# Two steps for the largest absolute K, six unread products, and the last segment turned by TensorE, under a new stored order

## The chip, the cores and the metric

The kernel runs on one core of one Trainium2 chip. Its engines work side by side, each through its own queue in order: TensorE (PE; its weight loads are listed as PEld), VectorE (DVE), ScalarE (ACT), GpSimd (POOL) and SyncE (SP, which here only issues DMAs). The metric is the device time of one execution in microseconds.

## The reference

Two independent layers on 2048 tokens of width 640; their outputs stand side by side. Layer A is a gated long convolution, layer B attention over four segments of 512 tokens with a memory carried between segments. Cut to what matters:

```python
# A: short filter on k (4 taps), times v, a causal convolution of length 2048 per channel, times q
k_shift = sum(k_pad[:, t:t + S] * shift_k[:, ks - 1 - t] for t in range(ks))
kv = k_shift * v
y = irfft(rfft(kv, 2 * S) * rfft(ssm_k, 2 * S))[:S] + kv * ssm_D
a = q * y
# B: 32 heads of 20, segments s = 0..3 of 512 tokens
q, k, v = x @ wq, x @ wk, x @ wv
p = softmax(qs @ ks.T * scale + causal_mask)
a_dot = p @ vs
a_mem = (phi(qs) @ M) / (phi(qs) @ z + 1e-6)      # phi(t) = t + 1 if t > 0 else exp(t)
o = g * a_mem + (1 - g) * a_dot                   # g = sigmoid(beta) per head
M, z = M + phi(ks).T @ vs, z + phi(ks).sum()
b = o @ wo
```

## The kernel before, in words

Layer A runs over five blocks of 128 channels (`conv`, `dp` 0 to 4). Each block loads and turns its filter, applies the short filter as seven shifted products with diagonal matrices (`ks`), multiplies by v (`vt`), transforms data and filter by products with cosine tables (`spectrum`: eight groups of four products into PSUM, each evicted by ACT to `F`, then sums and differences on DVE), multiplies the spectra on DVE (`product`: many `tensor_tensor` of 1024 to 4096 elements per partition), transforms back (`inverse`: eight products per piece, then a DVE product with q, then two stores from POOL's queue). The per-channel weight `ssm_D` enters as one extra product in the filter's first spectrum piece (line 459), with `Drow`, a tile that is zero but for the weights in its first row, and a tile of ones.

Layer B runs over eight units: segment `u // 2`, half of the heads `u % 2`. `project` computes K, Q and V for four groups of 128 tokens (five accumulating products of 320 columns each), evicts them by ACT, turns K and Q together by a DMA transpose on SP into `KQT` (a head takes 32 rows, 20 of them used), and forms phi of both. For the softmax no maximum over the scores is taken. Instead each query gets an upper bound: the largest absolute K of every channel (`kam`, line 608), spread into a small matrix `A`, times the absolute turned Q (`qabs`); four small products give the bound, ACT evicts it to `bT`, and four small DMAs on SP write it into spare rows of the turned Q, so that the score products subtract it.

`attend` computes the scores in three kinds of blocks: A and J below the diagonal, D on it (with the mask added by further products). Four score tiles run side by side in the array, since a head has only 32 rows. ACT takes the exponential of 1024 columns at a time into one of seven `ET` buffers (160 times in all); then value products of 21 columns sum the result in PSUM, DVE divides (`rr`, `o2`) and writes `o_s`. `project_out` turns `o_s`, multiplies by `wo` and stores. For segments 0 to 2 the turn is a DMA transpose. For segment 3 the five blocks of 128 columns are treated in three parts (`PARTS`): the first three blocks by one DMA transpose for each group of 128 tokens, the fourth ("mid") and fifth ("last") by PE products with the identity matrix and an eviction that alternates between ACT and DVE. The first part needs the heads of the last unit's first group, the last part needs the very last heads.

The order of the work is not the order of the program. A recorder lists every operation (1501 of them, line 147) and every PSUM group, and `issue` (line 244) emits them in a stored order, a permutation packed into a text (`ORDER`, line 775); a second text (`BASE`, line 797) gives each PSUM group its bank out of eight. The planner that found the order is not part of the kernel; its costs are in `price` (line 190) and have no effect on the stored order. All instructions carry the line number 253 in the profile, for they are issued there; the tiles' names tell them apart. Each engine takes its operations strictly in the stored order, and an operation whose inputs or bank are not ready holds up everything behind it on its engine.

Of the kernel before, what the change touches and what calls it, by code (L numbers as in the profile page):

```python
# [104 lines left out]
class Recorder:  # L105
# [84 lines left out]
    def price(self, op, method, out, ins, dur):  # L190
# [8 lines left out]
        elif method in ("dma_start", "dma_start_transpose"):  # L199
# [3 lines left out]
            if method == "dma_start_transpose":  # L203
                packets, per = size / 256, 23.5
                op.dur = 5.1 * size / 1024
# [56 lines left out]
class Layer:  # L262
    def __init__(self, ctx, tc, A_q, A_k, A_v, A_shift_k, A_ssm_k, A_ssm_D, B_x, B_wq, B_wk, B_wv, B_wo, B_beta, out):
# [52 lines left out]
        nc.gpsimd.dma_start(out=self.Drow[0:1, :], in_=self.ssm_D[None, :])  # L316
# [61 lines left out]
    def conv(self, dp):  # L378
# [56 lines left out]
        def spectrum(kind, src):  # L435
            F = self.ring("F", [128, 4, 2, 512], n=FBUF)
            summed = kind == "X" and dp in PEX
            for c in range(4):
# [4 lines left out]
                for i in range(2):  # L443
                    if i % FW == 0:
                        g = self.group(FW, "F")
                    with rec.one():
                        for j in range(2):
# [3 lines left out]
                            for h in range(2):  # L451
# [6 lines left out]
                                if last and h == 0:  # L458
                                    nc.tensor.matmul(o[:, 0:128], lhsT=self.ones[:], rhs=self.Drow[:, dsl], start=False, stop=False, grp=g, skip_group_check=True)
# [84 lines left out]


# [23 lines left out]
    def project(self, u):  # L569
# [5 lines left out]
        for t in range(4):  # L575
# [17 lines left out]
            for i, n in ((0, 4), (1, 2)):  # L593
# [135 lines left out]
    def project_out(self, s):  # L729
# [4 lines left out]
        for p in parts:  # L734
            for t in range(0, 4, n):
                rec.key = ("oT", s, t) + (() if p.stop == 5 else ("first",) if not p.start else ("mid",))
                o = self.o_s[s][:].rearrange("p t h d -> p t (h d)")
                if p.start:
# [4 lines left out]
                    self.evict((t + (p.stop == 5)) % 2, oT[:, t, p], g.ap[:, 0, 0:128 * (p.stop - p.start)].rearrange("p (c q) -> p c q", q=128), g)  # L743
# [29 lines left out]
SK_ACT, X_ACT, W_SP = (), False, ()  # L773
KQW, FW, WW = 1, 1, 1
ORDER = r"""
c-jrrgLW7S5Cy>9yLan0we8flZKt+v+qP{dwQbwBZR@>nm~$qrq!5vG5?#_uJc%qRC6#25jFMUcC9_PI88TBKCNU8~;z~pb5S6b&2``x>jpUL@5?>NX42dbRB(@}!#FA7JNiwM<NhG<XMHO+0h1`-&
(jkjfm8=p?vP%LaL=MR*$&mtCkQLeRT`Ef=e3QgThB%TEv5^XCP)G_(5h*GKq@a|N(vnB=N(m_`#iY38ll)Rf%1U}<KxU*yAmShilA^Z6M;$3AHKmqRlOU-saS;z0kqI@Vu{4o}(pnlxC@C)$rGnI#
Hqu<`$~<W)4Wy~mlk8|Ap(Tv8k^&fjoM<LJkpsEV3%PL<c~B5-rJW2!d+8vZWE_U0qm0K0OhZ0&k<OAAQ6#F2L{}+<Q5cJ<7=*#-jXvlm6EF-DF&(2Z2K_Mwvt_R2M_H6dIdqr8=pnN(1HEJjW@0G5
qc7^A9~!`I5<=Nz{6G;D!v}oC94U%V_>2e^(duKCL^m_qLM%d0`H3I$3;z(#!dnzuEK6ke|Af7zugt*$%*8@kB&ARqWw2D1$$VKL^AT3mqFNsrD#N6oR6s>6MkTD2Xf_Y9^%BEY$p%?28)b!Tl7?uE
{!$zz@l!U-02wHQqy}oD7HXpoN+71Kl}4zHDu`uOQ4LKHgu1AXb+Sd8Vz@Lzh^&zjvRZ<rIliDR+MzvKpcVe2CB9*Z43@3Z0Y@dQZIkWN5u>CvcF0aSD7z%G?Unr!PTF9kbjBe$ES<1Vy5P8U#cnwu  # L780
-OwF><d+<gV{%eX$ZzR^J#t#A>sOqTB{(Bz<(x#a0Q-$UI4>9El7zM}wg&6a(pp(3>uj+tuB}BE>uPbVkzJI=*3Oz+Z|h@&t%3ElB$m`#STAd618lrZka!l~5?gyqXvwUDtwu*1XrpC}jFSX5S*Az`
f^iUsa9OU%dL**3vH?`rNixWW*kNphsOkz#lT}!Wzw%Fp8nm`9#WI-I)8sbHuF7&um20vCJFyG9F;Vs)j7HF~8c}b^b-5`~HJXOfy$G$hB%I!s=o(&QXk?9~QM8T*XkFch$8rFhuo+vh72EJcj$l6;
>QOY(V>pGTdKzc39p`WyZLPmGvpaGgXK(@CteM`Ei?}O~<RtpqLpgyAmeG3HWn95kTtj#3XRR%hwXy4HVwZ3O59GeY)LUq32{o3cwRD!=5^Hizp^3D<p0NhnSd-{&G|`vxN?yxOeIs!+jV9ID8du|K
GQESlNMR{$q&<~q@?2g>DtnA4c!)=MinN+iQ)y}q)O0%BnrnK^Y+3Cd?&AUC>j=wY88oB*vrL*<v+5`tZDVb`J+&<Q%!FfXoTauj)=~qlmA26D_QN`AC;e*QEHrCsHp^}~ET`qQT-ILmS$^xFd-RRH
wU3tDYG^Ipss*f|6|th0#|qg;`6OTDt-O<BmQ4#=cKsl2wVig>E}B4#TMjK@IrTN(;In+P+?q@CXjko~`Lv|9);9XtUfFB=W4raQm9=tK-ty}+yq6bviMM!%=Xh+Ttc;bmC-w>xtb$dxDpu91S&&sU
r}3RtvYJNLvf5V1s#{&FVfE~#g<^fnt6@0NK3G^zvI6?s!n2@8WCRw{!usCYuq~h43!7roY^qgZRerI#Hs6|Zo+-g*Y{&L&&K8_ywYW>?*iWm?aGY*+INN60UM-^g^p{0qHO{cbw!|h|ab0T5te6(n
07heEF1HmHg>@OkMqFSG`5q;-q%N}38kGyJjF#2zy53gVY74dy+hCh)jjgouT29y6M%!$MwTJf99d<;kXeq6#TdbG%)}6M?`sh{*((Sg*_Ui%d#%g*{cUw(1<{{l@`|W@ow7z=CqI0P3wLNy!y6~8_
W&<|iaa(7H?Su`}&K#^m^rQ{cL3+ea*+?CwUD=(dtrO2$3=Y>G9HFCijP}>DI!*`ZHjT&ljLDX4#ql~pdvT&xXAMr$$vQ>ru|E5-1NSolPwR2*&Fy+ZPwFYn&NEs;r|D6xs8e;i&d?k@t2x<EXX-4S
t#fsb9@F!7!Om+(UeL>WMX%X)J7?$gqFu7fcE#rDRl8w*8JqnWhjDp>H`$Z@dDCuLWxdAh9KetK#DpBgL`=;4+@TNnlmod`Z`&QaYxnHFC1Fxl(qz1-cNvTKcuAk|8B;MelQShB*h70{?-|H6Ov`jk
!4F)fulSmInUDFIff<>J3p6vcFg@pMR=(g%F4D!iL>KCJUe#+_fCX8I*Y$?p(!wmtBFx1+ys7uKxaVeBmScH7)(R}f;(VyzSb`P#KufX|pXeif%o6^NPxY?e(`<aMFSIo8=rb+prTn$N(L#QQh5ajQ  # L790
`E%Cx;Vi>S9Kj#_$&sw$w^-F*>MQ-lKfKM~9Lw<>$K|?0SLsR}%)cDPe>AWBf5k)iR!4I=#o_PtgO1@^U8mDHoijL-Ls{N8=xv?F6<o<-Ea$WNUO(!3oxn+4t)CgJA^J%x_(Xo;WKLlNujEr%**EGY
{j5v4S-0q1F6BJV=K?O|GS1;5e$lV`P1oou26HtFctH<g4PV2xe8aa~$Fg42H*ym<a|^d}F}HC8ziVh;&oExyf9MYG<SrKTu)dpn7|tX3cJAd*-N$-f+RJ!-Kfv%F*$=XzH}YTVAfk9wZ|X%nq6c^#
uj`S#sMAAvV}Hm;tmZ-Pp2U-S6F<VE{H+x|nn(8-9@AraGmq`byt%jX*51-nd7!8ExE{~r`yWl<Ej*zo_mm#T6Zv0F>?e7O$9aP3J%wlT%$~)wdN$AQIXr`B^faE<5AiU&`acz<^PHZ`b9)}o>-jvt
clS2l&5zL#3ZVhC^>#keNBL;K%qzS|#c5t*d+*@k5FQcG(K~r(@8UhYr$<CoL_>7MKyUBkeZ8Oe_W?f8m-`qGgO%RP2l-$h;zNCy5BC*5!pHhJAMa;4!6*7zUgad8?B}@5&oeBhcqB~q=|00}`YfOA
0hr@+eV$+T>psor`vPC+i+r)K@m0Rg*ZUG*>#O~gAN9z%;lUo_SNyau^@D!MkNFng>YIGCpYtd<?-#huxBCX)=!gBdpYS7o#xM9uzv;L9s_*cNzSH;kHNWj={gUtXeZI?g`+h&*{{i6J>gE
"""
BASE = r"""
c-l=<0TRO?2#W~v{~r%R?7UtrB7_jE0XXn_vsQ;8%HCM?M0v7&S^L>p#c!S+o}I@7Ms@D4r;$)Gp@^V8p00sf7crc9MwDS=s?|&yHF(x6yH0Ws?gry9BUw2WW3-N#Z}ONm#jmTSSOx2Vh{m<m06m~(
{C1_W?mAZ2UWyK343ANEGxHE<D{eFMb~-f{tzc%VtLc16<0QLaU(VhjT`#N4_s}-^OkSs+CdDt}7GH?d?e22EI=Ha#b?)MLgp``gDCyrMl70Vqy7JGXtAChBvq)*Uc(TMa^qrdpX*;h!{hN?o7&GHw
tt3i{H;DLh`eWHMAOBQvRU9pyx<da-NK4n9_J@fH9gpYQn>RIeLzCE{=>tDfMh1%  # L800
# [8 lines left out]
def kernel(  # L809
# [63 lines left out]
```

## Time and profile before

| | |
|---|---|
| median of three runs | 290.04 us (289.86 to 291.36) |
| profiled execution | 290.99 us, its span 289.2 us |
| granted TensorE clock, mean | 0.987 |
| PE busy | 258.5 us, 4226 products |
| DVE busy | 262.0 us, 398 instructions |
| ACT busy | 254.0 us, 391 instructions |
| POOL busy | 42.5 us, 71 instructions |
| ACT's exponentials | 160, 155.9 us |
| DVE's reductions of the turned K | 8, 18.2 us |

Busy time is the time in which an engine has at least one instruction under way. Successive instructions of an engine can overlap a little, so the distance between two starts is often shorter than the first one's duration. A value in brackets at the end of a line of the timeline is the idle time before the instruction, with what ended it.

### The profile page before, as it was taken

To read this page: it belongs to the slowest core of one execution; us is meant where nothing else is said; L and a number is where in the kernel's file an instruction comes from. 1 tells how busy PE (TensorE), PEld (TensorE's weight loads), DVE (VectorE), ACT (ScalarE), POOL (GpSimd) and SP (SyncE) were. 2 spreads that over 40 slices of the span, in tenths; PEclk is the share of its full clock that TensorE was granted. 3 is DMA by queue.
4 is the path that set the end of the run, shared out by engine and by line. 5 is a ranking of instruction groups with operands and counts; after the bars stand their busy time and mean duration, and the time that the engine had idled before them with its cause. 6 is when DMAs were issued, how large, how long until landed. Compare 5 with 4: busy or idle time off the path is not lost. (4 is left out here: it accounts for less than half of the span.)

```text
span 289.2 us, 9883 instructions
## 1 busy us (share of the span) xinstructions
PE 258.5 (89%) x4226; PEld 195.3 (68%) x4226; DVE 262.0 (91%) x398; ACT 254.0 (88%) x391; POOL 42.5 (15%) x71
## 2 busy tenths in 40 slices
PE   0999998789989899999989999998799977888895
PEld 0788756668667678777656888656586755656673
DVE  0569999999999999999999999999999999989554
ACT  1694899899998978999999999999979999989972
POOL 8300000001005000403100310022001220001620
PEclk9999999999999989999999999999799999999999
DMA  6999889899943779916696149952492029921252
GB/s 190 383 243 178 217 160 174 207 215 164 223 118 85 165 99 204 205 61 120 166 167 144 43 59 174 191 133 71 88 156 57 24 55 141 207 26 48 58 123 91
DMA packets 113500, 40.71 MB, mean 141 GB/s; under 512 B 105696, under 2 KB 111376, under 8 KB 113328
## 3 DMA queue, kind: packets, MB, share of 16 engines
q1 hardware_dynamic: 108624, 34.07, 61.8%
q0 software_dynamic: 2064, 4.76, 5.5%
q10 hardware_dynamic: 2768, 1.24, 1.8%
q8 instruction: 33, 0.54, 0.8%
q14 instruction: 11, 0.09, 0.1%
HBM read 14.11 MB, written 5.24 MB: 67 GB/s over the span
## 5 line engine op out<-in xcount | busy, mean ns | idle before, releaser
L253 ACT ACTIVATE ET<-ps 128x1024 bf16<-128x1024 f32 x160 | 155.9, 1064 | 6.7 <-PE ps L253 6.4
L253 PEld LDWEIGHTS <-xT 128*128 128x128 bf16 x640 | 60.5, 99 | 32.2 <-issue 10.8
L253 PE MATMUL ps<-wqkv,xT 128*128 128x320 bf16 x480 | 75.5, 303 | 3.6 <-ACT ET L253 1.9
L253 ACT CAST F<-ps 128x512 bf16<-128x512 f32 x80 | 43.0, 614 | 4.2 <-DVE F L253 1.6
L253 POOL DMA_DIRECT2D out_dram<-outa x32 | 22.2, 815 | 165.1 <-DVE outa L253 141.1
L253 PEld LDWEIGHTS <-ET 128*128 128x128 bf16 x1296 | 40.3, 97 | 4.1 <-issue 2.2
L253 PE MATMUL ps<-Va,ET 128*128 128x21 bf16 x1280 | 41.2, 172 | 0.1
L253 PE MATMUL ps<-KQT 32*128 32x128 bf16 (+2 forms) x896 | 34.5, 242 | 2.0 <-ACT ET L253 1.0
L253 PEld LDWEIGHTS <-Wf 128*128 128x128 bf16 x320 | 29.9, 98 | 6.5 <-issue 2.4
L253 ACT CAST KQ<-ps 128x320 bf16<-128x320 f32 x64 | 27.5, 454 | 3.7 <-PE ps L253 3.1
L253 PE MATMUL ps<-wo,xT 128*128 128x320 bf16 x160 | 25.2, 299 | 1.1 <-ACT ET L253 0.6
L253 PEld LDWEIGHTS <-KQT 32*128 32x128 bf16 x896 | 16.5, 94 | 12.0 <-issue 10.8
L253 PE MATMUL ps<-skd,kr 128*128 128x128 bf16 (+3 forms) x140 | 20.9, 301 | 1.1 <-ACT ET L253 1.0
L253 PE MATMUL ps<-Y,Wi 128*128 128x256 bf16 x160 | 20.3, 273 | 1.7 <-ACT ET L253 1.0
L253 PE MATMUL ps<-vt,Wf 128*128 128x256 bf16 x160 | 20.1, 272 | 1.8 <-DVE vt L253 1.4
L253 PE MATMUL ps<-kT,Wf 128*128 128x256 bf16 x160 | 21.2, 276 | 0.0
L253 PEld LDWEIGHTS <-kr 128*128 128x128 bf16 x140 | 17.3, 146 | 5.5 <-issue 2.7
L253 DVE TENSOR_TENSOR o<-ps,rr 128x640 bf16<-128x640 f32 x24 | 19.7, 823 | 0.7
L253 PE MATMUL ps<-mright,mleft 32*128 32x128 bf16 x512 | 14.4, 219 | 6.5 <-ACT ET L253 3.4
L253 PE MATMUL ps<-Mbd,PqT 128*128 128x84 bf16 x96 | 18.2, 202 | 1.9 <-ACT ET L253 0.9
L253 DVE TENSOR_TENSOR Y<-Y,pq 128x2048 bf16<-128x2048 bf16 (+1 forms) x20 | 18.6, 949 | 0.1
L253 DVE TENSOR_TENSOR pq<-Xh,Kh 128x2048 bf16<-128x2048 bf16 x15 | 18.3, 1223 | 0.4
(77 smaller groups left out, 356.4 us busy)
## 6 DMA issues: line engine op xcount, KB each, us to landing
vt<-in_A_v_dram SPq DMA_DIRECT2D x10, 256.0 KB
pq<-in_A_q_dram SPq DMA_DIRECT2D x10, 256.0 KB
out_dram<-outa POOLq DMA_DIRECT2D x32, 64.0 KB, 2.5
out_dram<-outb POOLq DMA_DIRECT2D x12, 160.0 KB, 3.1
ET<-in_A_ssm_k_dram SPq DMA_DIRECT2D x3, 512.0 KB
Wf<-c_wf SPq DMA_DIRECT2D x2, 512.0 KB
Wi<-c_wi SPq DMA_DIRECT2D x1, 1024.0 KB
kT<-in_A_ssm_k_dram SPq DMA_DIRECT2D x2, 512.0 KB
```

The lines of the kernel that those rows point to most:

```text
L253: f(*[fix(a) for a in args], **{k: fix(v) for k, v in kw.items()})
```

## The change

- The largest absolute K is no longer reduced from the turned K. DVE takes the absolute value of the unturned K (a bit mask over 4 x 320 elements per partition), the maximum of token groups 0, 1 with 2, 3, and the maximum of the two that remain, written with zeroed pads into a new tile `kmax`. Four PE products with the identity turn it into a PSUM bank, and the reduction runs over that bank, 128 elements for each of four head groups. `qabs` and the rest stay.
- In segment 3 the first three blocks, too, are turned by PE (three products for each of four groups of 128 tokens) and evicted by DVE. Four DMA transposes leave SP's queue.
- Six products of the identity with 512 columns of `wo` write a PSUM bank that nobody reads (`keep_busy`).
- `Drow` becomes 128 by 128 with the weights of the five blocks in its rows 0 to 4; the product that adds them takes as its stationary operand one column of the identity repeated 128 times, and the tile of ones goes.
- The planner's cost of a DMA transpose gets a floor. This line acts on the planner alone.
- Both stored texts are new, for 1543 operations and 488 PSUM groups (470 before).

Unpacked and laid beside the old one, the new order has these marks. On PE, unit 2's turn of `kmax` stands among the second block's filter spectrum, unit 4's and 5's shortly after score and value products, unit 6's after a J block, unit 7's among V projections. Four of the unread products (2, 0, 3, 5) stand among the third block's data spectrum and unit 1's last score blocks, ahead of the fourth block's short filter; two (1, 4) stand between unit 5's last value products. At the start two more Q projections stand ahead of the first filter spectrum, the three new DVE steps of unit 0 ahead of its sums, one small `Mbd` product behind them. At the end one output projection of segment 2 moves from before the last inverse piece to between the last two groups of value products, and all eight three-product pieces of segment 3's projection come after the last value products, where before two of them came ahead. On SP, ACT, DVE and PE many neighbouring operations have changed places besides. The core of the diff:

```diff
-        self.Drow = c.tile([128, D], bf16, name="Drow")
-        self.ones = c.tile([128, 128], bf16, name="ones")
+        self.Drow = c.tile([128, 128], bf16, name="Drow")
+        self.kmax = c.tile([128, 16, 32], bf16, name="kmax")
...
-        nc.gpsimd.memset(self.ones[:], 1.0)
+        nc.gpsimd.memset(self.kmax[:, :, DH:32], 0.0)
...
-                                    nc.tensor.matmul(o[:, 0:128], lhsT=self.ones[:], rhs=self.Drow[:, dsl], ...)
+                                    nc.tensor.matmul(o[:, 0:128], lhsT=self.ident[:, dp:dp + 1].to_broadcast([128, 128]), rhs=self.Drow[:], ...)
...
+    def keep_busy(self):
+        for n in range(KEEP):
+            self.rec.key = ("keep", n)
+            g = self.group(1, "keep")
+            self.nc.tensor.matmul(g.ap[:, 0, :], lhsT=self.ident[:], rhs=self.wo[:, n % 5, 0:512], start=True, stop=True, grp=g)
...
+        rec.key = ("kmax", u)
+        ka = self.ring("qabs", [128, 4, L])[:].rearrange("p g q -> p (g q)")[:, 0:1280].rearrange("p (t h d) -> p t h d", t=4, h=16)
+        V.tensor_scalar(out=ka.bitcast(i16), in0=KQ[:, :, 0, :, 0:DH].bitcast(i16), scalar1=0x7fff, scalar2=None, op0=ALU.bitwise_and)
+        V.tensor_tensor(out=ka[:, 0:2], in0=ka[:, 0:2], in1=ka[:, 2:4], op=ALU.max)
+        V.tensor_tensor(out=self.kmax[:, :, 0:DH], in0=ka[:, 0], in1=ka[:, 1], op=ALU.max)
+        g = self.group(1, "kmax")
+        with rec.one():
+            for k in range(4):
+                nc.tensor.matmul(g.ap[:, 0, 128 * k:128 * k + 128], lhsT=self.kmax[:, 4 * k:4 * k + 4, :], rhs=self.ident[:], start=True, stop=True, grp=g)
         rec.key = ("bound", u)
         kam = self.ring("kam", [128, 4], f32, n=2)
-        V.tensor_reduce(out=kam[:], in_=KQT[:, 0], axis=AX.X, op=ALU.max, apply_absolute_value=True)
+        V.tensor_reduce(out=kam[:], in_=g.ap[:, 0, :].rearrange("p (k t) -> p k t", k=4), axis=AX.X, op=ALU.max, grp=g)
...
-                if p.start:
+                if len(parts) > 1:
                     g = self.group(1, "oT")
...
-                    self.evict((t + (p.stop == 5)) % 2, oT[:, t, p], ...)
-                elif len(parts) > 1:
-                    nc.sync.dma_start_transpose(out=oT[:, t, p], in_=o[:, t, 128 * p.start:128 * p.stop])
+                    self.evict(not p.start or (t + (p.stop == 5)) % 2, oT[:, t, p], ...)
...
+KEEP = 6
...
+    K.keep_busy()
```

More of the change, by code (lines that the diff above doesn't have):

```diff
@@ L204, in price @@
                 packets, per = size / 256, 23.5
-                op.dur = 5.1 * size / 1024
+                op.dur = max(1260, 5.1 * size / 1024)
                 op.lat = 1250.0 + (800.0 if dram else 0.0)
@@ L458, in spectrum @@
                                 if last and h == 0:
-                                    nc.tensor.matmul(o[:, 0:128], lhsT=self.ones[:], rhs=self.Drow[:, dsl], start=False, stop=False, grp=g, skip_group_check=True)
+                                    nc.tensor.matmul(o[:, 0:128], lhsT=self.ident[:, dp:dp + 1].to_broadcast([128, 128]), rhs=self.Drow[:], start=False, stop=False, grp=g, skip_group_check=True)
                     if i % FW == FW - 1:
@@ L742, in project_out @@
                             nc.tensor.matmul(g.ap[:, 0, 128 * (cc - p.start):128 * (cc - p.start) + 128], lhsT=o[:, t, 128 * cc:128 * cc + 128], rhs=self.ident[:], start=True, stop=True, grp=g)
-                    self.evict((t + (p.stop == 5)) % 2, oT[:, t, p], g.ap[:, 0, 0:128 * (p.stop - p.start)].rearrange("p (c q) -> p c q", q=128), g)
-                elif len(parts) > 1:
-                    nc.sync.dma_start_transpose(out=oT[:, t, p], in_=o[:, t, 128 * p.start:128 * p.stop])
+                    self.evict(not p.start or (t + (p.stop == 5)) % 2, oT[:, t, p], g.ap[:, 0, 0:128 * (p.stop - p.start)].rearrange("p (c q) -> p c q", q=128), g)
                 else:
@@ L779 @@
[L779 to L786, printed above, removed]
@@ new lines @@
+FD<BLwX^)zZZccC%Q&5_Go-v$)N<NWdPpysqZKp~BeReEkOdl!;rT;<YA7kD#Z^g`P$3wCQ5cnB*iaj5ST5I?Y@~B_p03b1oG<gWw+xnr8j^Emfh^K_vREr=Ul}5cWr-}5D!NF1%2KVYO*9l^v9>PL
+CE8!=XkA?@vDs8Zv!2%1xNM*$wV5uHeiDxZBmoCWe3sJ9Qd-x_dRZqcWtCLbYPwOXYYp8Z8>E9a*G<w<TWU=WmRdScT4+M9mNha|mdgqmCL^Sk4wp9CNfWWNcG0eSP`1i8X{~MbpSIK1jKPT9A=_oA
+?2<ovQVvUd?WWzehX&YFS88baBfI60{MFO4UyevGJs^8zuN;@e?5#=IhCw_k`(%}#krQ%Cj!9DfmS1vK&PiYP<9Ug|XpGJal8kNHjz;H2xg=Y3n|5MncHvg-%E27Mo}4I?Bso*C7gI77({Q71)=iq0
+qnM7p*@x*lnj>YDjFz!7PR7e+NzI`g#xd;A2{M3FWU`FoSSpC|oWSk6Lk)kW8pg;@J*kciJgtISn8;K5PbLvKpa*rGuGf$_q=z*WLSutoktnE(Ft{oKFc1kLa73dbGFIy~IjWNx0c&-Q-jJ|}i0cv_
@@ new lines @@
+wGo7yvP%&NhdS7;d-Rx|(7n1(Z^>iXuNFA2XEYFKfG2WW8se;8(sO!6uj)0ut~d0up4VVr(2LrGBY8)<aX4@4UAd)Aa9eXRH}A<Ey{q?h1e+oc@5>|U$nLza4<rEwauD0|fj-hZ?7)W-4bc%3^-v$#
+84r!n7(0=JIhhFYkq}Sir96{Y@<v|E3wbVykpxNcSTiycU+OE3f!K(JWO%KaIfYaCM&D{&q`-7O)8t5r=Q@pPkQS*>1F4Y?)$v51YI<bE49;X;=3`B4MMw)}bD5vB`G<cwi(mOdzfp~r0hzD|aS&u#
+n3Vy`#<$W8&Cvo8EQCe3ck)5rO92*SAr@v!bU<cwL=l=5XHk~m9F}A$mSbstlwvHyPm%>$kqz0A6FHCz6<Cp<<%^VOWmaN13va(zh1K|*Uo{WD>1S4Db=Kr({i0v^PHXUkzSocXN!y?;LR&3{wc4!9
+di=?<%#Fwfo5%WWz=n)!olq1-P=`&}h)vmy&DnyD*^*H#nzf?ae0D}&gs~WwAFa?D`4H1$TVcepg80rKjBD*s2wkuXyRm@n(G`ohgo_!=2HGHtXpyV{dRap2ZS8F}*YF?3npp>1%jVYK+FCmsU@fer
@@ L800 @@
-tt3i{H;DLh`eWHMAOBQvRU9pyx<da-NK4n9_J@fH9gpYQn>RIeLzCE{=>tDfMh1%
+c-l=<2@-@b42n7b|Kp87>rO{ob3te{b1O4Evn%Y`mHXZM<-1<Xti@o-eFr?Vr^4>A7d(lKT1)K;<vn-?JCOppwf;eD;AHZrJcdfXXI36miM5Av5<58)lQ^-fVRi7H%drtvh<K6ST$iWORl@(GJMv9W
+B4gl5Y4+yPe~=1YCO8f}tjrp&crr^x`o(h9K5Pd3OsAGcjqVC;AK;{vH`G4}CX5fAsD^lxnxmem46**XQG-AoyEPiUwAh*^hBr@dh+!$N#lgiPZnu6_2(fEab@gJpztL@<`#Sn_mN>}=#l-vIQiX(K
+k7g^NZGqi@F_j%D%~?DAOsu|&DK+{kU0|0|f;y)DlT)W}*7@o`1vs^Rl{wQo@;`Ty6L-(Qt~L2TW;X`U
 """
```

29 lines of the change are left out of this document (14 added, 15 removed).

## The prediction

> **What bounds the kernel now.** I read the busy times first, then the kernel in stretches, then the chain of waits, then single engines in order of time. The profiled execution took 290.99 us, its span is 289.2 us; the median of three runs is 290.04 us, 0.95 us less. All terms below are made against the profiled execution and the sum is then lowered by 0.95 us.
>
> The table by stretches has, after the length, the busy us of PE, weight loads, VectorE (DVE), ScalarE (ACT) and POOL, each with its number of instructions, then the granted clock.
>
> ```profile
> PE 258.5 (89%) x4226; PEld 195.3 (68%) x4226; DVE 262.0 (91%) x398; ACT 254.0 (88%) x391; POOL 42.5 (15%) x71
> ...
> 21.20:115.80 94.60, 88.46 (x1253) 67.69 (x1251) 93.47 (x135) 82.00 (x131) 5.59 (x8) 0.98 0.85 170
> 115.80:206.20 90.40, 84.92 (x1399) 62.78 (x1397) 89.56 (x129) 87.10 (x140) 15.49 (x24) 1.00 0.68 127
> 206.20:217.00 10.80, 10.80 (x179) 8.51 (x179) 10.66 (x19) 8.90 (x16) 0.00 (x0) 0.84 0.85 124
> 217.00:243.00 26.00, 22.29 (x488) 16.95 (x490) 25.36 (x40) 26.00 (x36) 5.52 (x8) 1.00 0.37 63
> 243.00:258.60 15.60, 13.12 (x303) 9.47 (x306) 14.55 (x23) 14.25 (x17) 0.00 (x0) 1.00 0.84 132
> 258.60:277.60 19.00, 16.62 (x373) 12.16 (x366) 14.30 (x26) 18.86 (x22) 5.83 (x9) 1.00 0.24 63
> 277.60:289.20 11.60, 8.40 (x136) 6.61 (x135) 5.70 (x15) 4.43 (x10) 1.95 (x3) 0.96 0.32 95
> ```
>
> The page's 91, 89 and 88 per cent look like three equal engines; the stretches do not. From 21.2 to 206.2 us DVE idles 1.13 + 0.84 us out of 185, so it sets the pace there. ACT idles 12.6 us before 115.8, but only 3.3 + 1.9 + 0 + 1.35 = 6.55 us from there to 258.6, and 0.14 us in the 19 us after. The end hangs on PE, as the chain of waits shows (start, length, what):
>
> ```profile
> 206.20 10.80 PE ps L253 x178
> ...
> 275.61 1.98 ACT ET L253 x2
> 277.59 0.04 issue
> 277.63 8.42 PE ps L253 x136
> 286.05 0.02 issue
> 286.07 0.43 ACT kT L253
> ```
>
> So: DVE until about 206, one PE piece, ACT's exponentials from 243 to 277.6, then 8.42 us of gapless PE. Work saved on DVE counts fully early, and later only as far as ACT can follow; work added in the last 8.42 us of PE counts in full.
>
> **The largest absolute K (eight times).** One reduction over 2048 turned elements of K goes. In its place come an absolute value of 1280 elements, a maximum of 640, a maximum of 320, four PE turns of 128 columns, and a reduction of 512 elements out of PSUM. Groups of DVE by shape (count, busy us, mean ns):
>
> ```profile
> L253 DVE TENSOR_REDUCE kam<-KQT 128x4 f32<-128x2048 bf16 x8 | 18.2, 2279 | 0.0
> L253 DVE TENSOR_SCALAR qabs<-KQ 128x1280 bf16<-128x1280 bf16 x6 | 2.8, 470 | 0.2
> L253 DVE TENSOR_TENSOR PP<-PP,qabs 128x640 bf16<-128x640 bf16 x12 | 5.8, 480 | 0.0
> L253 DVE TENSOR_TENSOR o_s<-o 128x320 bf16<-128x320 bf16 x24 | 7.1, 296 | 0.2
> L253 DVE TENSOR_TENSOR vt<-ps,vt 128x512 bf16<-128x512 f32 x20 | 13.1, 681 | 0.1
> ```
>
> The first three new steps have rows of their own size and pattern (the 1280-element row reads this same KQ layout). No reduction reads PSUM in this trace. Its lower end is a quarter of 2279, 570 ns; its upper end the same length read from PSUM beside a second operand, 681 ns; I take 0.68, the row nearest in source and length. What counts is the distance between starts:
>
> ```profile
> 29.12 2.28 DVE L253 TENSOR_REDUCE kam<-KQT 128x4 f32<-128x2048 bf16 x1
> 31.32 0.68 DVE L253 TENSOR_SCALAR qabs<-KQT 128x2048 int16<-128x2048 int16 x1
> ...
> 92.77 0.48 DVE L253 TENSOR_TENSOR PP<-PP,qabs 128x640 bf16<-128x640 bf16 x1
> 93.17 0.68 DVE L253 TENSOR_TENSOR vt<-ps,vt 128x512 bf16<-128x512 f32 x1
> 93.77 0.68 DVE L253 TENSOR_TENSOR skd<-ident,skc 128x512 bf16<-128x512 bf16 x1
> ```
>
> Each starts 0.08 us before the record in front ends (29.12 + 2.28 against 31.32; 92.77 + 0.48 against 93.17). So the old reduction occupies 2.20 us and the new four (0.47 + 0.48 + 0.30 + 0.68) - 4 x 0.08 = 1.61 us: 0.59 us saved per unit. A rule speaks against four for one: the Trainium skill, "VectorE: DVE Perf Modes", section "The DRAIN you can't avoid", says that the next op waits until the pipe is empty, and to keep the count of ops low (it adds that an op which is not held may start earlier). With whole records, 1.93 against 2.28, the six units would give 2.10 us and not 3.54, and the forecast, the other terms kept, would be 288.8 us; the starts above speak for the overlap.
>
> By the unpacked order, units 1 to 6 take this in the stretch that DVE bounds or shares: 6 x 0.59 = 3.54 us. Unit 0's first three steps now stand ahead of the first spectrum's sums, where DVE waits 1.73 us, and cost nothing (1.01 us); there the gain is 2.20 - 0.60 = 1.60 us. Were that wait gone, they would cost 1.01 us. Unit 7's lies after 243, under ACT: nothing. Together 5.14 us.
>
> **The start.** PE and ACT now take two more Q projections ahead of the first spectrum, and one small Mbd product falls behind it.
>
> ```profile
> 14.90 0.27 DVE L253 TENSOR_TENSOR Mbd<-ginv,epsrow 128x16 bf16<-128x16 f32 x1
> ...
> 21.19 1.23 DVE L253 TENSOR_TENSOR Kh<-F 128x2048 bf16<-128x2048 bf16 x1 [1.73 <-ACT F L253]
> ...
> 16.50 0.73 ACT L253 CAST KQ<-ps 128x320 bf16<-128x320 f32 x2
> 17.14 4.01 ACT L253 CAST F<-ps 128x512 bf16<-128x512 f32 x8
> ```
>
> Two evictions take ACT from 16.50 to 17.14, 0.64 us, in front of eight spectrum evictions that pace themselves; the product is 0.27 - 0.08 = 0.19 us. Cost: 0.83 us. On the load queue of SP one filter is swapped for another ahead of the tables: same bytes, zero. POOL's zeroing is reordered with one tile narrower and one new: zero, POOL being idle 85 per cent; if late, KQ's first transposes wait for it.
>
> **The rest of the new order.** Elsewhere neighbours change place on every queue, many DVE and PE operations by one to ten places beyond the shift of the insertions; the exponentials keep nearly their sequence. Nothing in the trace prices that. With ACT only 6.55 us idle between 115.8 and 258.6, units 3 to 6 (4 x 0.59 = 2.36 us) ask ACT for about a third of its idle time; I take a third of that gain, 0.79 us, as given back. Its ends are 0 and 2.36.
>
> **The last segment.** Four DMA transposes on SP leave, with no one queued behind them but the last stores; twelve PE turns and four DVE evictions of 384 columns come. PE in order of time at the end, and SP's row:
>
> ```profile
> 275.20 0.85 PE L253 MATMUL ps<-wo,xT 128*128 128x320 bf16 x5
> ...
> 278.81 0.99 PE L253 MATMUL ps<-wo,xT 128*128 128x320 bf16 x6
> 279.64 0.20 PE L253 MATMUL ps<-Mbd,PqT 128*128 128x84 bf16 x1
> ...
> 280.81 0.33 PE L253 MATMUL ps<-ident,o_s 128*128 128x128 bf16 x3
> 280.97 1.11 PE L253 MATMUL ps<-wo,xT 128*128 128x320 bf16 x7
> ...
> 273.14 6.18 SPq L253 DMA_TRANSPOSE xT<-o_s  x4
> ```
>
> A turn costs (280.97 - 280.81) / 3 = 0.05 us, twelve 0.64 us. All twelve stand ahead of the last value products, where PE waits for ACT (PE 16.62 of 19.00 us); without that cover they cost the 0.64. The old order filled the wait for the last exponential (278.81 to 279.64) with two three-product pieces of the last projection. The new one fills it with an older segment's projection, taken out of the gap at 275.20, and one block's turns. So all eight such pieces now follow the last values: 0.83 us more in the gapless tail. The four evictions lie on a DVE that is busy 5.70 of 11.60 us there: zero, else at most 4 x 0.68 us.
>
> **The six unread products and PE's other new work.** They write a free PSUM bank and nobody waits for them; PE would wait for the bank's last reader, an exponential or a spectrum eviction. Four stand around old time 97, two around 237.
>
> ```profile
> 97.20:100.60 3.40, 2.47 (x61) 1.84 (x59) 3.37 (x6) 3.40 (x6) 0.00 (x0) 1.00 0.45 101
> 100.60:104.00 3.40, 3.40 (x42) 2.09 (x42) 3.40 (x6) 2.40 (x3) 0.00 (x0) 0.50 0.64 141
> 203.00:206.40 3.40, 1.98 (x61) 1.15 (x62) 3.40 (x6) 2.93 (x5) 0.00 (x0) 1.00 0.35 79
> 206.40:209.80 3.40, 3.40 (x57) 2.38 (x46) 3.40 (x6) 3.40 (x5) 0.00 (x0) 0.50 0.57 73
> ...
> L253 PE MATMUL ps<-skd,kr 128*128 128x512 bf16 x20 | 8.2, 410 | 1.1 <-ACT ET L253 1.0
> ```
>
> Twice a stretch with a thinner PE (2.47 and 1.98 of 3.40 us) is followed by one at half clock. Half clock for 3.4 us loses 1.7 us of PE. At 100.6 DVE was busy throughout (3.40 of 3.40), so curing it gains nothing that ends last; at 206.4 the lost 1.7 us lie inside the PE piece of the chain, but no new product stands ahead of that. I take zero. Six products cost at most 6 x 0.41 = 2.5 us of PE, the 32 turns of K 32 x 0.05 = 1.7 us, both beside a DVE that is fuller; with DVE no longer the bound they would be paid.
>
> **Sum.** -5.14 + 0.83 + 0.79 + 0.83 = -2.69 us: 290.99 to 288.30 profiled, 287.4 us against the median.
>
> **Rivals.**
>
> *ACT takes over.* The late gain is hidden wholly: only 1.60 + 2 x 0.59 - 0.83 = 1.95 us arrive at 115.8, less 0.83 in the tail: 288.9 us. For it: ACT's 26.00 of 26.00 us from 217. Against: the 5.2 us idle before that.
>
> *DVE waits for the turned K.* The reduction now waits for a PE turn, and DVE takes its queue in order: the spectrum and product steps behind it stand still, and PE and ACT after them. In unit 6 only a sign mask and a 320-element sum (0.68 + 0.32 - 0.16 = 0.84 us) stand between the last maximum and the reduction, in unit 5 a reciprocal and a product. The turn stands behind whole score or projection pieces (0.85 us, row at 275.20). Seven units at a mean wait w cost 7w: the gain is gone at w = 0.38 us. At 0.75 us the time is 287.4 + 5.25 = 292.6 us. For it: the short cover in units 5 and 6; against: units 0, 2 and 3, with ten operations or more between.
>
> *The clock stays full.* If the shifted schedule and the products avoid both half-clock stretches, 1.7 us leave the chain's PE piece: 285.7 us. For it: products stand just ahead of the first such stretch; against: none ahead of the second. The Trainium skill, "TensorE: Matmul & The Clock Gate", section "Why this matters for your kernels", asks only for no PE gap above about 3 us; by it no product is needed and this case has no chance. The rows disagree: the clock halved with PE 73 and 58 per cent busy just before.
>
> **How the numbers follow.** Forecast 0.49, full clock 0.14, ACT 0.20, waiting DVE 0.17. Half a per cent of 290.04, 1.45 us, is about what a measurement of this kernel can tell: faster (under 288.6) 0.63, same 0.20, slower (over 291.5) 0.17. The range runs from 284.5, the full-clock case with ACT giving back nothing and a little more, to 291.5, where a waiting DVE (w = 0.58) begins to count as slower; about 0.15 lies outside. For the gain alone, 285 to 289.
>
> **What would show it.** Right: DVE's busy time about 4 us lower before 243, PSUM reductions near 0.68 us without idle time before them, the first spectrum sum near 21.9, a gapless PE tail near 6 us after the last value products. Wrong: DVE idle before the reductions, released by PE; ACT idle growing after 115; new half-clock stretches; PE waiting for a bank in front of the unread products.

## The result, and the profile after

The changed kernel takes 289.08 us (median of 20 runs, 288.18 to 290.88), the kernel before on the same chip 291.26 us (20 runs, 289.46 to 293.25): a ratio of 0.9927, 95% interval 0.991 to 0.9944, so 2.1 us faster. The prediction had 2.69 us less. The profiled execution of after is the slowest of its 20, at 290.88 us; why is told below.

The page of after, its busy times first, then stretches with the edges of the prediction's table up to 258.6, and later edges where its last exponential lies:

```profile
PE 262.8 (91%) x4276; PEld 198.1 (69%) x4276; DVE 260.8 (90%) x426; ACT 253.4 (88%) x391; POOL 42.3 (15%) x71
...
21.20:115.80 94.60, 89.71 (x1280) 69.32 (x1278) 92.49 (x145) 82.60 (x133) 5.58 (x8) 1.00 0.93 169
115.80:206.20 90.40, 87.11 (x1421) 64.61 (x1419) 89.21 (x139) 87.00 (x141) 14.53 (x22) 1.00 0.68 125
206.20:217.00 10.80, 9.97 (x177) 7.62 (x176) 10.63 (x20) 10.31 (x18) 1.07 (x2) 1.00 0.94 166
217.00:243.00 26.00, 23.81 (x509) 17.45 (x511) 25.66 (x45) 25.71 (x35) 5.54 (x8) 1.00 0.34 54
243.00:258.60 15.60, 14.25 (x307) 9.95 (x294) 14.95 (x27) 15.58 (x19) 0.00 (x0) 1.00 0.77 137
258.60:276.10 17.50, 15.57 (x366) 11.73 (x366) 12.62 (x24) 17.17 (x20) 5.81 (x9) 1.00 0.17 53
```

DVE has 28 instructions more and 1.2 us less work, and is as full as before. Both half-clock stretches are gone (1.00 in every row). The new steps by shape (count, busy us, mean ns, then idle time in front):

```profile
L253 DVE TENSOR_REDUCE kam<-ps 128x4 f32<-128x512 f32 x8 | 5.5, 684 | 0.1
L253 DVE TENSOR_SCALAR qabs<-KQ 128x1280 int16<-128x1280 int16 x8 | 3.9, 482 | 0.1
L253 DVE TENSOR_TENSOR qabs<-qabs 128x640 bf16<-128x640 bf16 x8 | 3.9, 481 | 0.0
L253 DVE TENSOR_TENSOR kmax<-qabs 128x320 bf16<-128x320 bf16 x8 | 2.6, 320 | 0.1
```

The reduction out of PSUM, which no row of the kernel before shows, took 0.684 us against 0.68 assumed, and DVE stood 0.1 us in front of all eight. The rival of a DVE that waits for the turned K did not happen.

To compare like with like, a second trace of the new order is wanted: that of the kernel without the unread products (first experiment), whose PE got its full clock at the same moment as the kernel before. Three landmarks of each, from the timelines: first spectrum sum on DVE; last exponentials on ACT (start, length); last stores on SP. Before:

```profile
21.19 1.23 DVE L253 TENSOR_TENSOR Kh<-F 128x2048 bf16<-128x2048 bf16 x1 [1.73 <-ACT F L253]
276.51 3.02 ACT L253 ACTIVATE ET<-ps 128x1024 bf16<-128x1024 f32 x3
284.72 2.13 SPq L253 DMA_DIRECT2D out_dram<-kT  x4
```

The new order without the unread products:

```profile
22.02 1.23 DVE L253 TENSOR_TENSOR Kh<-F 128x2048 bf16<-128x2048 bf16 x1 [0.96 <-ACT F L253]
272.46 3.79 ACT L253 ACTIVATE ET<-ps 128x1024 bf16<-128x1024 f32 x4
281.52 2.97 SPq L253 DMA_DIRECT2D out_dram<-kT  x4
```

After:

```profile
23.62 1.23 DVE L253 TENSOR_TENSOR Kh<-F 128x2048 bf16<-128x2048 bf16 x1 [0.99 <-ACT F L253]
275.00 2.89 ACT L253 ACTIVATE ET<-ps 128x1024 bf16<-128x1024 f32 x3
283.16 2.97 SPq L253 DMA_DIRECT2D out_dram<-kT  x4
```

| part of the span, us | before | without unread products | after | forecast of the difference |
|---|---|---|---|---|
| to the first spectrum sum | 21.19 | 22.02 (+0.83) | 23.62 (+2.43) | +0.83 |
| from there to the last exponential's end | 258.34 | 254.23 (-4.11) | 254.27 (-4.07) | -5.14 + 0.79 = -4.35 |
| from there to the end of the last store's issue | 7.32 | 8.24 (+0.92) | 8.24 (+0.92) | +0.83 |
| from there to the end of the span | 2.36 | 2.99 (+0.63) | 2.97 (+0.61) | 0 |
| span | 289.2 | 287.5 (-1.7) | 289.1 (-0.1) | -2.69 |

Three of the four rows came within 0.25 us of the forecast. The last row, a loss of 0.6 us, was not foreseen at all. And the first row of after is 1.6 us above that of its twin, which carries through to the end. Of this 0.36 us was there when PE began its first projection (10.48 us against 10.12). PE in order of time shows where most of the rest comes from: ten products of 320 columns took, after,

```profile
12.67 2.52 PE L253 MATMUL ps<-wqkv,xT 128*128 128x320 bf16 x10
15.27 1.52 PE L253 MATMUL ps<-wqkv,xT 128*128 128x320 bf16 x10
```

and in the twin

```profile
12.07 1.52 PE L253 MATMUL ps<-wqkv,xT 128*128 128x320 bf16 x10
```

In after's profiled execution the full clock came at 14.7 us, in the twin's and before's at 11.8 us. I put that down to the execution and not to the kernel, because the medians of the twin (289.31) and of after (289.08) agree; only one execution of each has a trace.

### The profile page after: what moved, and what is told of

Read it like the earlier page. It is cut to its first block, busy times and chain, and to the rows that moved or that the text cites. A ratio compares the mean times of both kernels' runs of the same rounds, so it can differ in the third digit from the quotient of the medians.

```text
span 289.1 us, 9977 instructions
## 1 busy us (share of the span) xinstructions
PE 262.8 (91%) x4276; PEld 198.1 (69%) x4276; DVE 260.8 (90%) x426; ACT 253.4 (88%) x391; POOL 42.3 (15%) x71
## 4 chain that ended last, share of the span: by engine, by line
PE 32%; DVE 27%; ACT 26%; issue 7%; DMA 4%; SPq 2%; DVEq 0%; ACTq 0%
PE ps L253 32%; ACT ET L253 18%; DVE Y L253 5%; DVE Xh L253 4%; ACT F L253 4%; DVE pq L253 3%; DMA Y<-in_B_x_dram 3%; DVE o L253 2%; DVE outa L253 2%; ACT KQ L253 2%; DMA KQT<-KQ 2%; DVE Kh L253 2%; SPq L253 2%; DVE qabs L253 1%; DVE kT L253 1%
## 5 line engine op out<-in xcount | busy, mean ns | idle before, releaser
L253 ACT ACTIVATE ET<-ps 128x1024 bf16<-128x1024 f32 x160 | 157.5, 1075 | 5.6 <-PE ps L253 5.1
L253 ACT CAST F<-ps 128x512 bf16<-128x512 f32 x80 | 43.7, 628 | 4.3 <-PE ps L253 3.4
L253 PE MATMUL ps<-vt,Wf 128*128 128x256 bf16 x160 | 21.2, 272 | 1.8 <-ACT F L253 0.8
L253 PEld LDWEIGHTS <-Wi 128*128 128x128 bf16 x160 | 15.2, 97 | 4.1 <-issue 1.7
```

The costliest lines, as they stand in the source:

```text
L253: f(*[fix(a) for a in args], **{k: fix(v) for k, v in kw.items()})
```

## The experiments

Every kernel computes the whole result; nothing is left out in any of them. Ratios are to the kernel before on the same chip, with their 95% intervals. The changed kernel stands at 0.9927.

### The unread products: taken out of after, put into before

```diff
-KEEP = 6
+KEEP = 0
```

> The changed kernel without its six unread products; everything else, the stored order too, as in the changed kernel. Theory (the gain is VectorE work saved by the two-step K maximum, less what start and tail cost): the same time as the changed kernel, about 289.1 us on its basis, within 0.8 us, whether or not a half-clock stretch comes back near 100 or 206 us. Rival (the gain is the full clock that the products keep): the two half-clock stretches of about 3.4 us come back, each takes 1.7 us of TensorE with it, and the time rises by 1.7 to 3.4 us, to about the time of the kernel before.

Measured: 289.31 us, ratio 0.9926 (0.9903 to 0.9949). One half-clock stretch came back, from 100.5 to 103.9 us, and it costs nothing that can be measured:

```profile
97.10:100.50 3.40, 2.62 (x60) 1.93 (x61) 3.37 (x7) 3.40 (x6) 0.00 (x0) 1.00 0.36 80
100.50:103.90 3.40, 3.04 (x62) 2.40 (x64) 3.40 (x5) 2.82 (x4) 0.00 (x0) 0.50 0.75 167
```

DVE is full in both rows (3.37, 3.40). The second stretch (206 us) stays away without the products, so it was not they that removed it.

In the kernel before, three products went into the stored order ahead of each half-clock stretch:

```diff
+    K.keep_busy()
```

> The kernel before with six unread products: three just ahead of where its first half-clock stretch lay (100.6 us), three around 203 to 206 us, ahead of the second. Theory: 0 to 0.5 us faster than before, because VectorE sets the pace at the first place and little of the second is on the path; the half clock may go or may move to another place. Rival (clock): both half-clock stretches go and the time falls by 1.7 us or more.

Measured: 293.02 us, ratio 1.0056 (1.0021 to 1.009). The second stretch went, the first stayed (100.0 to 103.4 us, clock 0.50). No gain in time; a small loss. Both theories missed here, the clock theory by more. But this run does not price the clock, because PE stood in front of the unread products until DVE had read the banks that they write (five of the six are in the trace):

```profile
L253 PE MATMUL ps<-wo,ident 128*128 128x512 bf16 x5 | 2.1, 422 | 3.7 <-DVE o L253 2.1 <-DVE o_s L253 1.6
```

In after that row has no idle time (0.0). So the products are worth nothing in the new order, and in the old one they cost more than they brought.

What the full clock itself is worth in the old order, the repeated executions of the kernel before tell in part. One half-clock stretch of 3.4 us lowers the mean clock of an execution by 0.006. Of the 74 executions of before that were timed beside these experiments, the 19 with a mean clock of 0.997 or more took 290.3 us on average, the 35 between 0.99 and 0.997 took 291.0, and the 20 below 0.99 took 291.4. Executions without half-clock stretches were 0.7 to 1 us shorter on average, though one of the four batches shows next to no difference. Whether the clock made them shorter, or an execution that is late for another reason leaves PE thinner and so loses the clock, was not tried.

### The reduction put back into the new order

```diff
-        V.tensor_reduce(out=kam[:], in_=g.ap[:, 0, :].rearrange("p (k t) -> p k t", k=4), axis=AX.X, op=ALU.max, grp=g)
+        V.tensor_reduce(out=kam[:], in_=KQT[:, 0], axis=AX.X, op=ALU.max, apply_absolute_value=True)
```

with the three DVE steps and the turn gone. Three placements were tried: where the new order has its reduction; in units 2, 5 and 7 later, beside the next step that reads the turned K; and with the bound's product on PE later as well.

> The changed kernel with one thing undone: the largest absolute K is again one VectorE reduction over the 2048 turned elements, at the same place in the order; the absolute value, the two maxima and the turns by TensorE are gone, the new order and the six unread products stay. Theory: seven units lose what the two steps saved, 1.6 us in the first and 0.59 us in each of six others, so about 4 to 5 us slower than the changed kernel and 2 to 3 us slower than the kernel before. Rival (the new order alone brings the gain): as fast as the changed kernel, within 0.8 us. In between, the difference is the net price of the two-step maximum under ScalarE's limit; 2.2 to 3.5 us would mean that ScalarE gives a part back.

> The changed kernel with one reduction over the turned K again, as in the earlier run, but in units 2, 5 and 7 placed later, next to the other step that reads the turned K, so that it does not stand ahead of K's transposes. New order and unread products stay. Theory: VectorE's wait for the transposes falls from 7.0 us to under 1.5 us, and what is left is the VectorE work itself: 3 to 6 us slower than the changed kernel, 1 to 4 us slower than before. Rival (the new order alone is the gain): within 0.8 us of the changed kernel.

> As the run before with one reduction in the new order, and in addition the bound's product on TensorE, its eviction and its row stores stand later in their queues (TensorE 0.9 to 3.0 us later by the trace), since TensorE stood 13.9 us at that product waiting for VectorE. New order and unread products otherwise. Theory (most of those 13.9 us only shift the wait; VectorE's longer reduction is the cause): TensorE's wait at the product falls to under 6 us, the time falls by 2 to 6 us against that run, and stays 4 us or more above the kernel before. Rival (it was the place of the product alone): within 2 us of the changed kernel.

Measured: 307.06, 302.23 and 304.65 us; ratios 1.0544, 1.0374, 1.0492 (each within 0.005). All far above the 2 to 3 us that the saved time would explain. The waits in front of the reduction and of the bound's product, in the first placement:

```profile
L253 DVE TENSOR_REDUCE kam<-KQT 128x4 f32<-128x2048 bf16 x8 | 18.3, 2281 | 7.0 <-DMA KQT<-KQ 7.0
L253 PE MATMUL ps<-qabs,A 128*32 128x512 bf16 x32 | 3.4, 417 | 8.8 <-DVE A L253 6.2 <-DVE qabs L253 2.5
```

and in the second:

```profile
L253 DVE TENSOR_REDUCE kam<-KQT 128x4 f32<-128x2048 bf16 x8 | 18.2, 2279 | 1.8 <-DMA KQT<-KQ 1.8
L253 PE MATMUL ps<-qabs,A 128*32 128x512 bf16 x32 | 3.4, 417 | 13.9 <-DVE A L253 13.9
```

The new order asks for the bound soon after the projections. The two-step maximum reads K before its DMA transposes; the old reduction must wait for them, and where it is placed behind them PE stands at the next product instead (after: 2.0 us there). Moving that product did not mend it either: PE's wait there fell to 1.3 us, and the time did not fall with it. So this order alone is not the gain: without the two steps it loses 10 us or more. These runs cannot price the reduction, though: they price an order made for another operation. An order laid out anew around the old reduction was not tried.

### The two-step maximum put into the old order

The three DVE steps, the turn and the short reduction as in after; no unread products; first blocks turned by DMA. (The new form of the `Drow` product stays in; its ten records take 2.2 us in either form.) First, with the turn right behind the last of the three steps in the list; then in seven units with the turn 1.3 us or more later by the trace, since K must be read before the next unit overwrites it (unit 4, which has no such room, keeps its reduction); last in units 0 to 3 alone:

```diff
+        if u < 4:
+            V.tensor_reduce(out=kam[:], in_=g.ap[:, 0, :].rearrange(...), axis=AX.X, op=ALU.max, grp=g)
+        else:
+            V.tensor_reduce(out=kam[:], in_=KQT[:, 0], axis=AX.X, op=ALU.max, apply_absolute_value=True)
```

> The kernel before with only the two-step K maximum put in: its old order, its first blocks turned by DMA, no unread products. Theory: 2 to 4 us faster than before (up to 5.1 us less ScalarE's share; the start and tail costs of the new order are not paid). Rival (the new order brings the gain, or VectorE waits for the turned K because the old order leaves it little cover): no gain, or slower, with VectorE idle in front of the reductions, released by TensorE.

Measured: 331.4 us, ratio 1.1371 (1.1335 to 1.1407). PE reached the turns long before DVE had the maxima:

```profile
L253 PE MATMUL ps<-ident,kmax 128*128 128x128 bf16 x32 | 3.6, 243 | 24.9 <-DVE kmax L253 21.1 <-DVE Va L253 2.8 <-ACT ET L253 1.1
```

> The kernel before with the two-step K maximum in units 0 to 3 and 5 to 7 (unit 4 keeps its one reduction), placed by the trace of before: its three VectorE steps early enough that the turn stands in TensorE's queue over 1.3 us behind the last of them, the reduction close to its old place; three sign steps move forward to free K in time. Old order otherwise, no unread products, first blocks turned by DMA. Theory (the saved VectorE time is the gain wherever the turn is given room): TensorE's idle time ahead of the turns falls from 24.9 us to under 3 us, and the time is 1 to 4 us below before. Rival (the old order has no room: K must live longer, so the next unit's evictions wait, and every engine's place is taken): no gain or slower, although TensorE no longer waits at the turns.

Measured: 295.5 us, ratio 1.0163 (1.0121 to 1.0204). PE's wait at the turns is down to 0.9 us, yet the kernel is slower than before: now DVE waits 3.8 us for the turned K, 2.2 us of it in unit 5, the wait that the prediction's rival described.

> The kernel before with the two-step maximum in units 0 to 3 alone, placed as in the run where TensorE did not wait at the turns; units 4 to 7 keep the one reduction. VectorE has 1.6 + 3 x 0.59 = 3.4 us less work before 125 us, and no wait was seen there at the turned K above 0.3 us. Theory of the prediction (VectorE sets the pace to 206 us, so its saved time counts in full early): 1.5 to 3.4 us faster than before. Rival (the old order holds the engines to one another, so that the saved time becomes idle time of VectorE): within 1 us of before, with VectorE's idle time up by about 2.5 us ahead of 155 us.

Measured: 290.63 us, ratio 1.0007 (0.9984 to 1.003). Up to 154.8 us, where only units 0 to 3 count, the old order and this kernel:

```profile
21.20:154.80 133.60, 125.74 (x1829) 94.61 (x1826) 132.16 (x188) 119.69 (x194) 13.34 (x20) 0.99 0.83 164
```

```profile
21.20:154.80 133.60, 125.37 (x1844) 94.93 (x1842) 129.13 (x198) 119.12 (x194) 13.32 (x20) 1.00 0.82 163
```

DVE lost 3.03 us of work and, the stretch being of fixed length, gained 3.03 us of idle time. That the same work was done by its end shows in a landmark there, the step behind unit 4's reduction, before and in this kernel:

```profile
154.76 1.22 DVE L253 TENSOR_TENSOR Xh<-Y 128x2048 bf16<-128x2048 bf16 x1
```

```profile
155.31 1.21 DVE L253 TENSOR_TENSOR Xh<-Y 128x2048 bf16<-128x2048 bf16 x1
```

It is later by 0.55 us, 0.43 of which it had at the first spectrum sum. DVE's waits there grew from 1.7 us (one wait, for ACT's `F`) to 4.2 us, ended by ACT's `F` and PE's pieces. The prediction's "work saved on DVE counts fully early" is wrong for the old order.

### The saved time put back into the new order

```diff
         V.tensor_scalar(out=qabs[:].bitcast(i16), in0=KQT[:, 1].bitcast(i16), scalar1=0x7fff, scalar2=None, op0=ALU.bitwise_and)
+        V.tensor_scalar(out=qabs[:].bitcast(i16), in0=KQT[:, 1].bitcast(i16), scalar1=0x7fff, scalar2=None, op0=ALU.bitwise_and)
```

> The changed kernel with VectorE given back what the two-step maximum saves: the step that clears the signs of the turned Q (0.69 us) runs twice in every unit, the second time over the same bytes, so 0.60 us more of VectorE per unit between two starts, with no new wait and nothing else moved. Theory (in the new order VectorE's time counts from unit to unit, less what ScalarE gives back late): 0.6 in unit 0, 6 x 0.60 in units 1 to 6, a third of units 3 to 6 hidden, unit 7 nothing: 2.8 to 4.2 us slower than the changed kernel. Rival (as in the old order, where 3 us less of VectorE changed nothing, its time is slack, and the gain of the new order comes from its sequence): under 1 us slower. Over 5 us would mean that the order is rigid and multiplies a delay, as in the runs with one reduction.

Measured: 294.79 us, ratio 1.0139 (1.0107 to 1.017). Against after that is 1.0139 / 0.9927 = 1.021, or 6.2 us, give or take 1 us by the two intervals. The second step cost more than the expected 0.60 us, for it writes the tile that the first one writes: it starts 0.04 us behind the end of the first one's record and not 0.08 us ahead of it. The twin without unread products, then this kernel:

```profile
32.11 0.68 DVE L253 TENSOR_SCALAR qabs<-KQT 128x2048 int16<-128x2048 int16 x1
32.71 0.28 DVE L253 TENSOR_TENSOR A<-sel,kam 128x128 bf16<-128x128 bf16 x1
```

```profile
32.53 1.41 DVE L253 TENSOR_SCALAR qabs<-KQT 128x2048 int16<-128x2048 int16 x2
33.86 0.28 DVE L253 TENSOR_TENSOR A<-sel,kam 128x128 bf16<-128x128 bf16 x1
```

From the first start to the step `A` it is 1.33 us against 0.60: 0.73 us put back per unit, 5.8 us in all. How it adds up shows in the first and last start of `A`. The twin, then this kernel (count, ns, first to last start):

```profile
L253 DVE TENSOR_TENSOR A<-sel,kam x8: 280/284/292, 32.7 to 246.0; 128x128 bf16<-128x128 bf16 x8
```

```profile
L253 DVE TENSOR_TENSOR A<-sel,kam x8: 279/283/292, 33.9 to 251.7; 128x128 bf16<-128x128 bf16 x8
```

It is late by 1.2 us in unit 0 (0.42 of which it had at the first spectrum sum) and by 5.7 us in unit 7: 4.5 us over seven units, on average 0.64 us of the 0.73 in each. The last exponentials (`272.45 9.40 ... x10` in the timeline) end at 281.85 us against 276.25, 5.6 us later. Less the 0.42 us of the start, 5.2 of the 5.8 us arrive there, nine tenths: ACT gave back hardly anything, and unit 7's step counts like the others.

One limit: the doubled step stands right ahead of `A`, for which PE's bound product waits, and PE's idle time there rose from 1.8 to 5.9 us. So the run lengthens the path from K to the bound together with DVE's work, and does not tell the two apart.

### The start and the tail

Two Q projections and their evictions moved behind the first filter spectrum; and, beside that, an older projection piece moved from 277 to 259 us and one three-product piece hoisted ahead of the last value products. Both are changes of the stored order alone.

> The changed kernel with two Q projections and their evictions moved behind the first filter spectrum, about as the kernel before has them. Theory (the start costs what stands ahead of the first spectrum, and VectorE sets the pace behind it): the first spectrum sum starts 1.3 us earlier for the same phase of the clock (two pieces of 0.68 us of TensorE), and 0.5 to 1.3 us of it arrive at the end. Rival (ScalarE's exponentials set the end, so an earlier start is given back): under 0.3 us at the end.

> The start as in the run beside it, and in the tail one older projection piece moved forward from 277 to 259 us, with one three-product piece of the last projection hoisted ahead of the last value products in its place. Theory: the gapless TensorE tail shortens by 0.4 to 0.6 us, so 1 to 1.8 us faster than the changed kernel, about 287.5 us. Rival: the moved piece delays scores near 260 us and ScalarE, which is full there, loses as much: no better than the start alone.

Measured: 289.74 us (0.995, 0.9928 to 0.9972) and 289.64 us (0.9951, 0.9927 to 0.9975): no better than after. The start did come earlier, at 21.26 us; but DVE then waited 1.4 us for PE's short-filter products, which now stand behind the two projections (0.2 us in the twin), and the second spectrum's sums began at 33.53 us against 32.91. In the tail kernel ACT stood 0.27 us more near 260 us, where it is full, and the last exponential ended 0.70 us later than in its companion (0.31 of it were there before that wait); from there to the last issue it was 0.45 us shorter. Both rivals had the size, the first with another place: the gain was given back at the second spectrum, not at the end.

Then the first blocks of the last segment turned by DMA again:

```diff
-                if len(parts) > 1:
+                if p.start:
...
+                elif len(parts) > 1:
+                    nc.sync.dma_start_transpose(out=oT[:, t, p], in_=o[:, t, 128 * p.start:128 * p.stop])
```

> The changed kernel with the first blocks of the last segment turned by four DMA transposes again, issued where the turns stood; nothing else moved. Theory (the turns cost what they take in TensorE's gapless tail, 12 x 0.05 us, and nothing on VectorE): 0.3 to 0.7 us less from the last value products to the last store. Rival (a transpose lands later than a turn's eviction, and TensorE waits for it in the tail): 1 to 3 us longer tail, with TensorE's idle time released by the transposes.

Measured: 288.79 us, ratio 0.9949 (0.9928 to 0.9969), not told apart from after. From the first product of the last value group to the start of the last store it took 7.75 us against 7.70 in the twin: the twelve turns cost nothing that their absence gives back. Nothing on PE waited for the four transposes either; the one wait for a transpose of `o_s` (1.0 us) lies near 117 us and belongs to segment 0. So both the theory and the rival missed.

## Why the prediction came out right, and where it was not

- **Size and direction.** 289.08 us against 287.4, inside the range, faster. The forecast stood on a median of 290.04 us; in the comparison the kernel before took 291.26, so the gain is 2.1 us against 2.69. Of the 0.96 us by which the twin's span (-1.73) missed the sum (-2.69), 0.63 lie behind the last issue, 0.24 in the middle, 0.09 in the tail; the start fitted. That the middle came so close is partly luck, as the next points show.
- **The start, +0.83.** Measured +0.83 at the same moment of full clock. In after's own trace it is +2.43; of the other 1.6 us, 0.36 were there at the first projection and the rest came with the later full clock.
- **The largest absolute K.** The durations were right (0.482, 0.481, 0.320, 0.684 us). The distance between starts was right only where another operation stands between two of the new steps. In after:

```profile
48.04 0.48 DVE L253 TENSOR_TENSOR qabs<-qabs 128x640 bf16<-128x640 bf16 x1
48.44 1.29 DVE L253 TENSOR_TENSOR Y<-Y,pq 128x1024 bf16<-128x1024 bf16 x2
...
244.07 0.48 DVE L253 TENSOR_TENSOR qabs<-qabs 128x640 bf16<-128x640 bf16 x1
244.59 0.33 DVE L253 TENSOR_TENSOR kmax<-qabs 128x320 bf16<-128x320 bf16 x1
```

  The first maximum takes 0.40 us to the next start when an unrelated step follows (unit 1), 0.52 when the second maximum, which reads its result, follows at once (units 0 and 7). In unit 4 the step `A` follows the reduction at once, with 0.72 us instead of 0.60. Added up over units 1 to 6 of the twin, the new steps take 10.03 us and the old reductions took 13.18: 3.15 us saved, not 3.54. With whole records and the other terms kept, the middle would have gained 1.60 + 2.10 - 0.79 = 2.91 us; it gained 4.11. The Trainium skill, "VectorE: DVE Perf Modes", section "The DRAIN you can't avoid", says that the next operation waits until the pipe is empty and that one which is not held starts earlier. It does not decide here: the trace has both kinds of start, and the four short ones take 1.70 us on average against 2.20 for the long one.
- **"Work saved on DVE counts fully early."** This step failed as stated. In the old order 3.03 us less work gave 3.03 us more idle time and no time at all. In the new order nine tenths of the time put back arrive at the last exponential. The 99% of DVE before 206 us did not say that DVE alone set the pace: with less work it waited for ACT's `F` and for PE's pieces instead. In the orders tried, the gain needs both parts, and neither alone has it: this order alone +3.7% at best, two steps alone +0.1% at best.
- **ACT gives back a third, 0.79; unit 7 gives nothing.** Both wrong, against each other: the time put back counted from unit 0 to unit 7, 0.64 us a unit on average, and ACT hid a tenth of it at most. By the starts in the twin the middle saved 1.60 + 3.15 + 0.42 = 5.2 us, nine tenths of which are 4.6; it gained 4.11. The half microsecond between was not located. Nor did the gain arrive where it was forecast. Counted by exponentials from the first spectrum sum, the twin led by 2.1 us at the end of the 120th of the 160 (239.4 us in the kernel before) and by 4.1 us at the end of the 140th (260.9 us): half of the gain came in the stretch around and behind 243 us, under ACT, for which the forecast had none. ACT's idle time from 243 to 258.6 us fell from 1.35 to 0.02 us by the rows; what let it do so was not tried.
- **The signs to look for.** The first spectrum sum near 21.9 us: 22.02 in the twin. No idle time in front of the reductions: so. ACT idle growing after 115 us would have been a sign against it; from 115.8 to 258.6 us ACT's idle time fell from 6.55 us to 4.2 (3.40 + 0.49 + 0.29 + 0.02 by stretches). But DVE's busy time before 243 us is 1.1 us lower and not 4 (219.05 and 217.99 by the rows of the four stretches). Between the two landmarks of the table it fell by 3.3 us (248.49 before, 245.19 in the twin), although three of the four new evictions of 384 columns (0.55 us each) lie there: saved time shows between landmarks, not between fixed edges.
- **The tail, +0.83.** Measured +0.92, gapless on PE from 277.63 to 283.67 us in the twin, as forecast (near 6 us). That the twelve turns, all ahead of the last value products, would be free was right.
- **The unread products, zero.** Right. The full clock came true (the rival at 285.7 us), but not by the products, and not with 1.7 us more of gain. That it is worth nothing is not shown: by the executions of the kernel before, up to about 1 us of the 2.1 us may go with it.
- **A DVE that waits for the turned K.** Not in the changed kernel; in the old order it came as described (3.8 us).

## What to carry over

A low idle share of one engine in a stored order tells that adding to it may cost, not that taking from it will pay: find what each other engine delivers just behind it, or count on laying the order out anew together with the operation. Price an operation inside the order it was made for; the same operation in the other order cost up to 40 us here because one engine reached a wait early. Take the distance between starts from a place where the operation stands as it will stand: directly behind the step that makes its input it cost 0.12 us more here. Compare two traces from the first common landmark on, part by part, so that a late clock at the start is not read as a loss of the change.

## What the runs showed of the hardware

- **The start of a DVE operation.** In the rows above, an operation that follows an unrelated one started 0.08 us before the record in front ended; one that reads, or writes again, what the one in front writes started 0.03 to 0.04 us behind that end (the two maxima of unit 7: 0.52 us from start to start for a record of 0.48; the doubled step: 1.33 us for two records of 0.68 and 0.69).
- **The start of the full clock.** PE's full clock began between 10.2 and 14.7 us in the traces of this study, and every later half-clock stretch ahead of the last stores lasted 3.4 us or a multiple of it. A start 2.9 us later went with a first spectrum 1.6 us later, 0.36 of which had another source, and all of it arrived at the end.
- **Half clock without a long gap.** After rows with PE busy 2.47 and 1.98 of 3.40 us (before) and 2.62 of 3.40 us (without unread products) the clock halved; no two starts of PE were more than 1 us apart in them. A low share is not enough, though: in the kernel before it stayed full behind a row with 2.02 of 3.40 us:

```profile
52.80:56.20 3.40, 2.02 (x45) 1.70 (x44) 3.29 (x6) 2.65 (x4) 0.00 (x0) 1.00 0.54 95
56.20:59.60 3.40, 2.87 (x80) 2.27 (x78) 3.37 (x6) 3.40 (x6) 0.00 (x0) 1.00 0.72 284
```

  The five traces of the new order with two steps and unread products have no half-clock stretch before the last stores, the one without has one. What decides is open.
- **A packet of the instruction queue at the end.** In after it comes behind the last store. The queues of after from 284 to 292 us:

```profile
q1 hardware_dynamic: 576, 0.66, 22.9%
q14 instruction: 1, 0.01, 0.3%
```

The kernel before shows none in the same window. After the last store's issue the spans run 2.36 us there and 2.97 us in after. The packet is not shown to be the cause. In both kernels the last store has landed 1.43 to 1.44 us after its issue, and 0.9 us pass from SP's last wait to the end. The difference lies between the two: SP's last wait is over 0.02 us after the landing in the kernel before and 0.63 us after it in after (288.19 us), and the packet starts only at 288.63 us. What holds SP there was not tried.
